# Window attention and FFN in one kernel: weight bits joined from a PSUM bank, a longer count for the turns, one copy at the end, a new table of offsets

## The chip, the cores and the metric

One core of one Trainium2 chip runs the whole program. Its engines are TensorE (PE, with its weight loads shown as PEld), VectorE (DVE), ScalarE (ACT), GpSimd (POOL) and SyncE (SP), which here issues nearly all DMAs. Each engine takes its own instructions in order and waits for the others through semaphores. The metric is device microseconds of one execution, as the median of three runs.

## The reference

`reference` computes attention over 8 batches and 8 heads of 64 columns, and feeds the result to a feed-forward network (FFN). Every head has 32 global and 512 local tokens. Global queries see all 544 keys; local queries see the 32 global keys and the local keys at most 32 places away.

```
s_g = scale * np.matmul(q_g, k_all.transpose(0, 1, 3, 2))
out_g = np.matmul(sm(s_g), v_all)
mask = np.abs(pos[:, None] - pos[None, :]) <= window
s_ll = np.where(mask, s_ll, -1000000000.0)
out_l = np.matmul(sm(np.concatenate([s_lg, s_ll], axis=-1)), np.concatenate([v_g, v_l], axis=2))
h = x @ w_in
g = h - np.tanh(h)
return (g @ w_out).astype(np.float32)
```

x is the attention output, 4352 rows of 512; w_in is 512 by 2048 and w_out 2048 by 512. Both weights come as 64-bit floats, the rest as 32-bit floats.

## The kernel before

**Precision.** Each factor of the FFN's matmuls is split into a rounded part and a remainder (hi and lo), and three products are added: hi by hi, hi by lo, lo by hi.

**Weights.** `add_weights` (L396) handles 32 pieces, 16 of w_in and 16 of w_out. A piece is loaded as 512 pairs of 32-bit words for each partition, into `wraw01` or, for every other piece, `first_q`. A buffer's next load waits until its piece has been joined. Four steps make one float of a pair: `rebias` on ACT (L429) rescales the upper word in place; `low` on DVE (L433) shifts the lower word by 29 places in place; `join` on DVE (L438) shifts the upper word by 3, ors both and writes `sq`; `high` on ACT (L364) rounds it into `w_in_hi` or `w_out_hi`, and `rest` (L444) subtracts that into `w_in_lo` or `w_out_lo`. Which engine subtracts, DVE or POOL, is the planner's choice.

**Attention.** Heads go in pairs, 32 in all, four to a batch. Pairs 0 to 3 are worked out by an older way: PE transposes keys and queries (L547), scores (L656), DVE finds peaks, ACT takes exponentials (L1111), POOL scales (L1117), PE transposes the probabilities (L1176), ACT or DVE stores them, and PE forms the products (L814). From pair 4 on the band scores come from L730, the exponentials from L1137, POOL scales (L1146), DVE turns blocks (L1152), DMAs put them in their places, and the products come from L814 up to pair 7 and L830 after. Values are loaded into one buffer, so a pair's values are loaded once the products before it are done. The scores of the global queries are made for two pairs at once (a quad, `L1030`, or `L972` from pair 8 on); their path is peaks (L982, L985), a swap of halves (L977), exponentials (L993), a second swap and reciprocal (L997, L998), scaling on POOL (L1003), and two turns on DVE, one for each head (L793 and L795), and then the products of the quad's first pair (L830).

**FFN.** Eight chunks of 512 local rows and a last one of 256 global rows. A step makes 128 hidden columns: 12 matmuls of 128 by 512 (L1219; the first four steps of batch 0 are written at L1245, so that they can begin with the first heads), tanh on ACT (L1227), a subtraction on DVE (L1230), rounding to `gates` (L364), the remainder (L1236, by DVE or POOL), and 12 more matmuls into the output (L1282). The hidden sums use PSUM banks 0 to 3, outputs 4 to 7, attention 0 to 2 from batch 1 on.

**Order.** Nothing is ordered by hand. `Order.run` is a planner: each operation states engines it may run on, with a duration and a penalty for each, a due time, what it reads and writes, and the banks it takes. The planner repeatedly takes the operation that could start first by its own reckoning. `lock` marks DVE operations that it will not overlap with POOL's. Due times, penalties and offsets come from the table `CFG`. When PE would be idle early on, the planner puts in matmuls without use, called fillers here (L1520). What it decides is fixed at build time: the chip sees plain queues, and banks are fixed with them.

Of the kernel before, what the change touches and what calls it, by code (L numbers as in the profile page):

```python
# [217 lines left out]
def kernel(ctx, tc, q_l, k_l, v_l, q_g, k_g, v_g, w_in, w_out, out):  # L218
    nc = tc.nc
    B, H, S, _ = q_l.shape  # L220
# [3 lines left out]
    DM, DFF = w_in.shape  # L224
# [11 lines left out]
    OWN = 8  # L236
# [94 lines left out]
    def bank(shape, j, dt=F32):  # L331
# [6 lines left out]
        elif len(shape) == 4:  # L338
# [4 lines left out]
    CFG = dict(a_g=-2.1233, a_kg=-0.0964, a_ph=-0.2641, a_qs=5.2608, a_w=-5.4882, a_wn=-5.0581, a_xg=150, d_g=3.6283, d_kg=1.9778, d_ph=50.4226,  # L343
               d_qh=26.732, d_qs=-7.1422, d_tg=0.8523, d_tp=37.2986, d_w=30.7139, d_wn=39.585, d_xg=38.7617, d_y=2.8076, gfirst=0, ho=5270.2449,
               hs=2156.5317, lag=1357.4346, last=1709.3, newb=2, p0=1360.6541, pen=53.0844, penp=52.559, s_g=-0.3344, s_w=0.027, step=4184.7811,
               step1=131.5084, lag0=-8364.46, hs0=1060.8452, tol=7.769536e-06, wd0=5841.993, wsp=-418.2128, xw=0.0005229852, o_ld0=7690.8676,
               o_tn0=177.2342, o_tg0=-8529.9354, o_s0=-8629.8545, o_sp0=-1339.9745, o_t0=-1524.9303, o_vl0=2302.8731, o_pv0=-5083.3973,
               wsp1=-52.8356, ho0=6811.9657, mw=0.141697, o_h0=-385.2625, hp=-7418.8823, bp0=8145.2771, bp1=-8139.4914, bp2=-3489.8108,
               bp3=-2305.7318, p_w=49.4081, p_kg=19.7546, mv=1.068302e-05, kd=2.127385e-05, a_sq=8.5297, o_gb=6064.0102, o_kl2=-2470.8967,
               o_ql2=2380.1114, o_kt2=930.5723, o_qt2=7843.6435, o_l2=-3985.7135, o_lp2=2466.9212, o_g2=-2616.5954, o_tg2=-354.9467,  # L350
               o_sq2=-3032.5223, o_vl2=-3610.1076, o_pv2=8733.5803, o_kl1=5682.2566, o_ql1=7667.6045, o_kt1=1958.0937, o_qt1=-6967.0531,
               o_l1=-6273.5988, o_lp1=7383.6579, o_g1=4840.8538, o_tg1=7460.9702, o_sq1=7629.0969, o_vl1=-2671.5821, o_pv1=-8776.7889,
               o_g0=-5078.2772, p_bd=49.2555)
# [4 lines left out]
    add = order.add  # L358
# [4 lines left out]
    def copy(e, dst, src):  # L363
        (nc.scalar.copy if e == "A" else eng[e].tensor_copy)(dst, src)  # L364
# [31 lines left out]
    def add_weights(n):  # L396
# [10 lines left out]
        box = {}  # L407
# [23 lines left out]
        def low(e, _):  # L431
            v = box["v"].bitcast(I32)
            nc.vector.tensor_scalar(v, v, 29, None, op0=ALU.logical_shift_right)  # L433

        def join(e, _):
            v, up = [box["raw"][:, :, k].bitcast(I32) for k in range(2)]
            box["v"] = flat
            nc.vector.scalar_tensor_tensor(box["v"].bitcast(I32), up, 3, v, op0=ALU.logical_shift_left, op1=ALU.bitwise_or)  # L438
# [61 lines left out]
    class Pair:  # L500
# [278 lines left out]
        def add_global_turn(self):  # L779
            for a in self.heads:  # L780
# [17 lines left out]
                add(("D", 1.65 if self.j >= OWN else 1.6), turn, self.due(self.C["o_tg"]), r=["pg0"], w=[f"hg{a.two}"])  # L798
# [391 lines left out]
    class Chunk:  # L1190
        def __init__(self, x, xkeys, n, name, dst, due):
            self.x, self.n, self.name, self.dst, self.due = x, n, name, dst, due
            self.hs = CFG["hs0"] if name == "b0" else CFG["hs"]
            self.per = 512 // n
            self.steps = NF // self.per
            self.xkeys = xkeys
            self.h, self.g, self.acc, self.final = {}, {}, None, False
# [69 lines left out]
        def add_out(self, s):  # L1267
# [31 lines left out]
            if last:  # L1299
                for tt in range(nt):  # L1300
# [14 lines left out]
                    if self.final and tt == nt - 1:  # L1315
                        def half(lo):
                            def fn(e, _, tt=tt, key=key):
                                copy(e, wraw[key[1]][:, lo:lo + DM // 2], self.acc[tt][:, lo:lo + DM // 2])
                            return fn
# [7 lines left out]
                    parts = [key, key + ("b",)] if self.final and tt == nt - 1 else [key]  # L1327
                    add(("S", 0.45 * k), out_dma(runs[:k]), due + 0.5, r=parts, w=[("out", self.name, tt)], xfer=0.78)
                    if runs[k:]:
                        add(("A", 0.45 * k), out_dma(runs[k:]), due + 0.5, r=parts, w=[("out", self.name, tt, 1)], xfer=0.78)  # L1330
# [183 lines left out]
    chunks[-1].final = True  # L1514
# [42 lines left out]
```

## Time and profile before

| | us |
|---|---|
| median of three runs | 920.47 |
| lowest and highest | 916.97, 920.97 |
| the profiled execution | 916.99 |
| its span in the trace | 915.2 |
| PE busy in the span | 895.0 |
| DVE busy | 550.6 |
| ACT busy | 386.2 |
| POOL busy | 204.3 |

The span runs from the first to the last instruction; the execution's own time is 1.8 us more. Times in the trace are counted from the span's start. A view by stretches gives the busy time of each engine between two moments; a timeline lists instructions with the idle time before them and what ended it; the chain of waits follows the last instruction back to what released it. A busy PE is not always one at work that is needed, since fillers count as busy, and its clock may be granted at one of two levels, 1.0 being 2.4 GHz and 0.5 being 1.2 GHz.

### The profile page before, as it was taken

The numbers are of one execution on the slowest core, as the hardware profiler recorded it, in microseconds if no ns is written. First come the engines' busy times: TensorE is split into PE (matmuls) and PEld (weight loads), VectorE is DVE, ScalarE is ACT, GpSimd is POOL, SyncE is SP. The second block draws the span as 40 slices with busy tenths as digits, with TensorE's granted clock in tenths as the row PEclk, the third lists the DMA queues.
The fourth block names the chain that finished last, engine by engine and source line by source line (L and its number), as shares of the span: only waits on it lengthen the run. The fifth ranks groups of instructions, "written<-read, shape, count | busy, mean of one in ns | idle before, by whom it ended". The sixth has DMA issues, their size and how long they took to land.

```text
span 915.2 us, 23456 instructions
## 1 busy us (share of the span) xinstructions
PE 895.0 (98%) x9109; PEld 720.6 (79%) x9109; DVE 550.6 (60%) x1916; ACT 386.2 (42%) x1078; POOL 204.3 (22%) x366
## 2 busy tenths in 40 slices
PE   8989999999999999999999999999999999999998
PEld 6757777787787878777787878777778878888896
DVE  6878878855848485575747485665847462222231
ACT  6976566433334343433334343533344332322221
POOL 5656654220113121221113121211102030000000
PEclk9999999999999999999999999999999999999999
DMA  9785674754545525554645536454555330100100
GB/s 202 181 211 172 182 185 117 179 123 105 123 105 134 144 58 128 128 111 110 127 107 131 136 65 147 120 110 101 124 120 129 94 93 1 47 1 1 45 2 23
DMA packets 286958, 101.13 MB, mean 110 GB/s; under 512 B 254848, under 2 KB 277376, under 8 KB 286848
## 3 DMA queue, kind: packets, MB, share of 16 engines
q1 hardware_dynamic: 284800, 98.53, 45.2%
q8 instruction: 71, 1.16, 0.6%
q10 hardware_dynamic: 2048, 1.11, 0.5%
q14 instruction: 39, 0.32, 0.1%
HBM read 76.01 MB, written 21.50 MB: 107 GB/s over the span
## 4 chain that ended last, share of the span: by engine, by line
PE 74%; DVE 16%; ACT 4%; DMA 2%; SPq 2%; issue 2%; POOL 0%; ACTq 0%; DVEq 0%; POOLq 0%
PE bank L1282 33%; PE bank L1219 31%; DVE turned L793 4%; PE bank L830 4%; PE bank L730 3%; DVE stats L977 2%; DVE t L1230 2%; SPq L752 1%; DVE sq L1152 1%; PE bank L972 1%; DVE sq L438 1%; DVE pg L982 1%; PE bank L1245 1%; ACT turned L364 1%; DVE turned L795 1%
## 5 line engine op out<-in xcount | busy, mean ns | idle before, releaser
L1282 PE MATMUL bank<-w_out_hi,gates 128*128 128x512 f32 x1088 | 299.3, 395 | 2.8 <-ACT gates L364 2.8
L1282 PEld LDWEIGHTS bank<-w_out_hi,gates 128*128 128x128 f32 x1088 | 200.8, 188 | 50.8 <-issue 5.0
L1230 DVE TENSOR_TENSOR t<-bank,t 128x512 f32<-128x512 f32 x136 | 92.9, 684 | 173.1 <-ACT t L1227 172.7
L1146 POOL TENSOR_SCALAR prob<-prob,stats 128x128 f32<-128x128 f32 x224 | 91.1, 425 | 457.6 <-DVE stats L1142 264.0
L1227 ACT ACTIVATE t<-bank 128x512 f32<-128x512 f32 x136 | 80.8, 596 | 234.1 <-PE bank L1219 233.7
L364 ACT CAST gates<-t 128x512 fp32r<-128x512 f32 x136 | 84.5, 622 | 197.1 <-PE bank L1282 126.0
L1282 PE MATMUL bank<-w_out_lo,gates 128*128 128x512 f32 x544 | 151.7, 393 | 0.1
L1236 DVE TENSOR_TENSOR gates<-t,gates 128x512 fp32r<-128x512 f32 x101 | 70.5, 698 | 100.0 <-PE bank L1282 91.2
L1219 PE MATMUL bank<-x_hi,w_in_hi 128*128 128x512 f32 x432 | 120.5, 395 | 0.0
L1282 PEld LDWEIGHTS bank<-w_out_lo,gates 128*128 128x128 f32 x544 | 102.5, 188 | 22.4 <-issue 0.3
L1219 PE MATMUL bank<-x_hi,w_in_lo 128*128 128x512 f32 x432 | 118.6, 390 | 0.0
L1219 PE MATMUL bank<-x_lo,w_in_hi 128*128 128x512 f32 x432 | 118.3, 390 | 0.0
L1219 PEld LDWEIGHTS bank<-x_lo,w_in_hi 128*128 128x128 f32 x432 | 81.0, 188 | 17.3 <-issue 0.2
L1219 PEld LDWEIGHTS bank<-x_hi,w_in_lo 128*128 128x128 f32 x432 | 80.6, 188 | 17.6 <-issue 0.2
L1219 PEld LDWEIGHTS bank<-x_hi,w_in_hi 128*128 128x128 f32 x432 | 79.6, 188 | 17.6 <-issue 0.6
L1137 ACT ACTIVATE prob<-prob,stats 128x128 f32<-128x128 f32 x224 | 86.9, 390 | 2.1 <-DVE stats L1132 2.0
L793 DVE STREAM_TRANSPOSE turned<-pg 32x96 f32<-32x96 f32 x288 | 77.5, 269 | 5.6
L1236 POOL TENSOR_TENSOR gates<-t,gates 128x512 fp32r<-128x512 f32 x35 | 46.1, 1319 | 47.2 <-PE bank L1282 25.7
L1152 DVE STREAM_TRANSPOSE sq<-prob 128x512 f32<-128x512 f32 x50 | 34.6, 703 | 33.5 <-POOL prob L1146 32.1
L1132 DVE CUSTOM_DVE_ANT_0 prob<-bank,band 128x128 f32<-128x128 f32 x224 | 49.4, 284 | 0.6 <-PE bank L730 0.5
L830 PEld LDWEIGHTS bank<-turned 128*32 128x32 f32 x3072 | 33.4, 111 | 13.1 <-DVE turned L795 8.5
L1137 ACT ACTIVATION_READ_ACCUMULATOR prob<-prob,stats 128x1 f32 x224 | 42.1, 188 | 0.0
(159 smaller groups left out, 935.4 us busy)
## 6 DMA issues: line engine op xcount, KB each, us to landing
moved<-sq SPq DMA_DIRECT2D x24, 512.0 KB, 3.0
turned<-in_v_l_dram SPq DMA_DIRECT2D x23, 512.0 KB, 5.5
turned<-in_v_l_dram SPq DMA_DIRECT2D x32, 256.0 KB, 3.4
out_dram<-wraw SPq DMA_DIRECT2D x32, 256.0 KB, 2.1
rawkq<-in_k_l_dram SPq DMA_DIRECT2D x112, 64.0 KB, 2.5
rawkq<-in_q_l_dram SPq DMA_DIRECT2D x112, 64.0 KB, 2.4
turned<-in_v_g_dram SPq DMA_DIRECT2D x48, 128.0 KB, 4.6
turned<-moved SPq DMA_DIRECT2D x48, 128.0 KB, 3.7
```

Source lines behind the costliest of these rows:

```text
L364: (nc.scalar.copy if e == "A" else eng[e].tensor_copy)(dst, src)
L793: nc.vector.transpose(win_g[G * g:G * g + G, a.two, 3 * x:3 * x + 3], view(pgh[r, a.two, G * (j + x):G * (j + x) + 1], [(3 * G, 3), (1, G)]))
L830: m = nc.tensor.matmul(y, win_v[:, NW * a.two + w, G * d:G * d + G], x, start=n == 0, stop=n == 7, skip_group_check=True)
L1132: nc.vector.tensor_tensor_reduce(out=x[:, t], in0=self.scores[:, t], in1=bands[0 if t == 0 else 2 if t == NT - 1 else 1], scale=-0.125, sc ...
L1137: nc.scalar.activation(x[:, t], x[:, t], AF.Exp, bias=self.st[:, t:t + 1], scale=-1.0, accum_out=self.st[:, 4 + t:5 + t])
L1146: nc.gpsimd.tensor_scalar(x[:, t], x[:, t], self.st[:, 8 + t:9 + t], 1.0, op0=ALU.mult, op1=ALU.mult)
L1152: nc.vector.transpose(z[:, :, self.two].rearrange("p n t c -> p t n c"), x[:, :, k * n * G:(k + 1) * n * G].rearrange("p t (n c) -> p t n ...
L1219: nc.tensor.matmul(self.h[s][:, j * n:(j + 1) * n], w[:, cc, f * P:(f + 1) * P], self.x()[xi](cc)[:, :n], start=part == 0 and cc == 0 and ...
L1227: nc.scalar.activation(tt_[q], self.h[s], AF.Tanh)
L1230: nc.vector.tensor_sub(tt_[q], self.h.pop(s), tt_[q])
L1236: eng[e].tensor_sub(gg[q][1], tt_[q].rearrange("p (k c) -> p k c", k=4), f32(gg[q][0]))
L1282: nc.tensor.matmul(self.acc[tt], g[:, j * nt + tt], low_out(f) if wi else w_out_hi[:, f], start=s == 0 and k == 1, stop=last and k == 3 * ...
```

## The change

Four things change. `low` no longer writes over the raw words: it takes a PSUM bank (any of the eight for the first eight pieces, later one of banks 0 to 3), writes the shifted bits there, and `join` reads them from it and gives it back. The planner's account is changed with it: `low` at 0.68 us instead of 0.48, `low`, `join` and DVE's subtraction no longer marked as locked against POOL, and the global turn from pair 8 on at 1.9 us instead of 1.65. The last chunk's last rows are copied out of PSUM by one instruction, where two copied a half each. And the table `CFG` has new values throughout, so the planner makes another order.

```diff
     def subtract(n, kind):
-        return [("P", (0.17 + n * 0.00218), 0.0), ("D", (n + 151) / 960, CFG.get("s_" + kind, PENP), True)]
+        return [("P", (0.17 + n * 0.00218), 0.0), ("D", (n + 151) / 960, CFG.get("s_" + kind, PENP), False)]
...
-        def low(e, _):
-            v = box["v"].bitcast(I32)
-            nc.vector.tensor_scalar(v, v, 29, None, op0=ALU.logical_shift_right)
+        def low(e, tags):
+            box["low"] = bank([P, 512], tags[low_]).bitcast(I32)
+            nc.vector.tensor_scalar(box["low"], box["v"].bitcast(I32), 29, None, op0=ALU.logical_shift_right)
...
-            nc.vector.scalar_tensor_tensor(box["v"].bitcast(I32), up, 3, v, op0=ALU.logical_shift_left, op1=ALU.bitwise_or)
+            nc.vector.scalar_tensor_tensor(box["v"].bitcast(I32), up, 3, box["low"], op0=ALU.logical_shift_left, op1=ALU.bitwise_or)
...
-            add(("D", 0.48), low, due, r=keys, w=keys, lock=True)
-            add(("D", 0.69), join, due, r=keys, w=[wj], lock=True)
+            low_ = ("low", n)
+            add(("D", 0.68), low, due, r=keys, w=[low_], alloc=[(low_, None if n < 8 else "h")])
+            add(("D", 0.69), join, due, r=keys + [low_], w=[wj], free=[(low_, 1)])
...
-                add(("D", 1.65 if self.j >= OWN else 1.6), turn, self.due(self.C["o_tg"]), r=["pg0"], w=[f"hg{a.two}"])
+                add(("D", 1.9 if self.j >= OWN else 1.6), turn, self.due(self.C["o_tg"]), r=["pg0"], w=[f"hg{a.two}"])
...
-                    if self.final and tt == nt - 1:
-                        def half(lo):
...
-                        add(("D", 0.42), half(DM // 2), due + 0.5, r=[acc], w=[key + ("b",)], res=[key], free=[(acc, 2)])
-                        add(("A", 0.37), half(0), due + 0.5, r=[acc], w=[key], free=[(acc, 2)])
-                    else:
-                        add(either(512, "y", True), out_copy, due + 0.5, r=[acc], w=[key], free=[(acc, 1)])
+                    add(either(512, "y", True), out_copy, due + 0.5, r=[acc], w=[key], free=[(acc, 1)])
...
-               hs=2156.5317, lag=1357.4346, last=1709.3, newb=2, p0=1360.6541, pen=53.0844, penp=52.559, s_g=-0.3344, s_w=0.027, step=4184.7811,
...
+               hs=1945.7008, lag=2058.0703, last=-656.3726, newb=2, p0=1174.4585, pen=-2.1431, penp=-16.7696, s_g=37.3966, s_w=10.8784,
```

**What the table does to the queues.** Counted over the whole program, all 136 gate subtractions (L1236) are on POOL, where 101 were on DVE; so are all 32 weight subtractions, where 9 were on DVE. The 28 copies of the global keys and four copies of the first global keys move from ACT to POOL. Four stores of the global turn, and the first store of the global keys and queries, move from ACT to DVE. There are 12 fillers instead of 21. Matmuls, exponentials and DMAs are as many as before.

On ACT, the rows ahead of the first tanh (`t_67<-bank`), before the change; `x_hi` is the products of the fourth pair, L429 is `rebias`, L1137 exponentials of batch 1:

```order
L1137 ACTIVATE prob_92,stats<-prob_92,stats 128x128 x4
L364 CAST w_out_hi<-sq 128x512
L364 CAST x_hi_75<-bank_105 128x256
L429 ACTIVATE wraw_64<-wraw_64 128x512
L364 CAST x_hi_75<-bank_101 128x256
L1137 ACTIVATE prob_93,stats<-prob_93,stats 128x128 x4
L364 CAST w_in_hi<-sq 128x4x128
L429 ACTIVATE first_q<-first_q 128x512
L1227 ACTIVATE t_67<-bank_102 128x512
L1227 ACTIVATE t_66<-bank_103 128x512
```

And after it:

```order
L428 ACTIVATE first_q<-first_q 128x512
L363 CAST x_hi_75<-bank_105 128x256
L363 CAST x_hi_75<-bank_104 128x256
L363 CAST w_out_hi<-sq 128x512
L428 ACTIVATE wraw_64<-wraw_64 128x512
L1227 ACTIVATE t_67<-bank_103 128x512
L363 CAST w_in_hi<-sq 128x4x128
L1227 ACTIVATE t_66<-bank_102 128x512
```

Both copies to `x_hi` now stand ahead of the rebias, and the eight exponentials behind the first tanh.

On SP, from the load of piece 8 into `wraw` to the load of piece 10 into it, before the change (`in_v_l`, `in_v_g` are values, `rawkq` raw keys and queries of batch 1):

```order
L418 DMA wraw_64<-in_moe_w_in_dram 128x4x256
L418 DMA first_q<-in_moe_w_out_dram 128x1024
L626 DMA turned<-in_v_l_dram 128x8x64
L626 DMA turned<-in_v_l_dram 64x8x64
L636 DMA turned<-in_v_g_dram 32x4x64 x2
L686 DMA rawkq<-in_k_l_dram 32x16x32 x4
L418 DMA wraw_64<-in_moe_w_in_dram 128x4x256
```

And after it (`qgt` is the global keys and queries):

```order
L417 DMA wraw_64<-in_moe_w_in_dram 128x4x256
L686 DMA rawkq<-in_q_l_dram 32x16x32 x4
L884 DMA qgt<-in_k_g_dram 32x4x32 x4
L626 DMA turned<-in_v_l_dram 128x8x64
L626 DMA turned<-in_v_l_dram 64x8x64
L636 DMA turned<-in_v_g_dram 32x4x64 x2
L417 DMA first_q<-in_moe_w_out_dram 128x1024
L884 DMA qgt<-in_q_g_dram 32x4x32 x4
L417 DMA wraw_64<-in_moe_w_in_dram 128x4x256
```

Counted from the first row of SP, four loads of raw keys fewer stand ahead of the load of piece 10.

On POOL, around the scaling for one quad of batch 2 (L1003), before the change:

```order
L1146 TENSOR_SCALAR prob_92<-prob_92,stats 128x128 x4
L1146 TENSOR_SCALAR prob_93<-prob_93,stats 128x128 x4
L1003 TENSOR_SCALAR pg<-pg,stats 128x288 x2
L1236 TENSOR_TENSOR gates<-t_67,gates 128x4x128
L1236 TENSOR_TENSOR gates<-t_66,gates 128x4x128
```

And after it:

```order
L1146 TENSOR_SCALAR prob_92<-prob_92,stats 128x128 x4
L1146 TENSOR_SCALAR prob_93<-prob_93,stats 128x128 x4
L1236 TENSOR_TENSOR gates<-t_66,gates 128x4x128
L1003 TENSOR_SCALAR pg<-pg,stats 128x288 x2
L1236 TENSOR_TENSOR gates<-t_67,gates 128x4x128
```

Around that quad, eight to ten gate subtractions (L1236) stand between one L1003 and the next, where one or two stood.

## Rows read from the trace of the kernel before

**Rows 1.** Busy us by stretch: length, then each engine (instructions), granted clock, DMA share, GB/s.

```profile
0.00:63.30 63.30, 53.90 (x453) 39.93 (x453) 47.96 (x202) 52.52 (x163) 34.25 (x67) 1.00 0.86 202
63.30:165.00 101.70, 99.91 (x757) 78.51 (x757) 87.25 (x276) 62.08 (x161) 59.55 (x70) 0.98 0.60 157
165.00:765.00 600.00, 595.21 (x7173) 478.26 (x7170) 378.26 (x1382) 234.77 (x694) 107.55 (x227) 1.00 0.50 116
```

**Rows 2.** Chain of waits in order of time, 52 to 58 us: start, us, what.

```profile
52.16 4.56 DMA wraw<-in_moe_w_in_dram
56.80 0.67 ACT wraw L429
```

**Rows 3.** Timeline of ACT: start us, us, instruction, count [idle before, releaser].

```profile
52.70 0.40 ACT L1137 ACTIVATE prob<-prob,stats 128x128 f32<-128x128 f32 x1
...
54.25 0.60 ACT L364 CAST w_out_hi<-sq 128x512 fp32r<-128x512 f32 x1
...
56.80 0.67 ACT L429 ACTIVATE wraw<-wraw 128x512 f32<-128x512 f32 x1 [1.68 <-DMA wraw<-in_moe_w_in_dram]
57.38 0.35 ACT L364 CAST x_hi<-bank 128x256 fp32r<-128x256 f32 x1
...
60.20 0.67 ACT L429 ACTIVATE first_q<-first_q 128x512 f32<-128x512 f32 x1
60.78 1.05 ACT L1227 ACTIVATE t<-bank 128x512 f32<-128x512 f32 x2
```

**Rows 4.** Timeline of PE around the first FFN steps, columns as in rows 3.

```profile
57.78 0.49 PE L1245 MATMUL bank<-x_hi,w_in_hi 128*128 128x512 f32 x1 [1.75 <-ACT x_hi L364]
...
63.46 1.30 PE L1282 MATMUL bank<-w_out_hi,gates 128*128 128x512 f32 x4 [2.43 <-ACT gates L364]
```

**Rows 5.** Granted clock of PE by stretch: length, PE busy, clock, DMA share, GB/s.

```profile
64.40:67.80 3.40, 3.40 (x10) 0.51 0.72 161
```

**Rows 6.** Timeline of the DMA queue of SP, columns as in rows 3.

```profile
49.06 3.00 SPq L686 DMA_DIRECT2D rawkq<-in_k_l_dram  x4
52.16 0.43 SPq L418 DMA_DIRECT2D wraw<-in_moe_w_in_dram  x1
```

**Rows 7.** Busy us of one line on DVE, L433, then L438, 0 to 165 us.

```profile
0.00:165.00 165.00, 19.91 (x32) 0.99 0.70 174
...
0.00:165.00 165.00, 26.83 (x32) 0.99 0.70 174
```

**Rows 8.** Line L438: duration ns min/median/max, first and last start.

```profile
L438 DVE SCALAR_TENSOR_TENSOR sq<-wraw x18: 650/694/1659, 8.8 to 148.5; 128x512 int32<-128x512 int32 x18
```

**Rows 9.** Groups by line and form, DVE, 0 to 165 us: busy, mean ns | idle.

```profile
L433 DVE TENSOR_SCALAR wraw<-wraw 128x512 int32<-128x512 int32 x18 | 11.7, 648 | 2.4 <-DMA wraw<-in_moe_w_out_dram 1.9 <-DMA wraw<-in_moe_w_in_dram 0.4
...
L364 DVE COPY first_q<-bank 128x512 f32<-128x512 f32 x4 | 2.7, 682 | 3.9 <-PE bank L547 3.9
```

**Rows 10.** Page, costliest groups: busy us, mean ns of one | idle before, releaser.

```profile
L1236 DVE TENSOR_TENSOR gates<-t,gates 128x512 fp32r<-128x512 f32 x101 | 70.5, 698 | 100.0 <-PE bank L1282 91.2
...
L1236 POOL TENSOR_TENSOR gates<-t,gates 128x512 fp32r<-128x512 f32 x35 | 46.1, 1319 | 47.2 <-PE bank L1282 25.7
```

**Rows 11.** Waits of PE: us in total, times, longest.

```profile
PE bank L830 <- DVE turned L795: 3.9, 11, 0.6
```

**Rows 12.** Timeline of one quad in batch 2, all engines, columns as in rows 3.

```profile
278.69 0.42 PE L972 MATMUL bank<-kw,qgt 64*32 64x256 f32 x4
...
283.17 1.13 DVE L977 COPY stats<-stats 32x2 f32<-32x2 f32 x4
...
289.62 0.20 DVE L795 STREAM_TRANSPOSE turned<-pg 32x32 f32<-32x32 f32 x1
...
289.88 1.33 PE L830 MATMUL bank<-turned 128*32 128x64 f32 x105 [0.27 <-DVE turned L795]
```

**Rows 13.** Timeline of the last rows' copies, columns as in rows 3.

```profile
909.61 0.59 ACT L364 COPY wraw<-bank 128x512 f32<-128x512 f32 x1 [4.42 <-PE bank L1282]
...
911.45 0.37 ACT L364 COPY wraw<-bank 128x256 f32<-128x256 f32 x1 [1.25 <-DVE wraw L364]
```

More of the change, by code (lines that the diff above doesn't have):

```diff
@@ new lines @@
+    CFG = dict(a_g=-20, a_kg=8.6471, a_ph=-0.3776, a_qs=3.1395, a_w=0.1186, a_wn=0.3468, a_xg=106.4499, d_g=3.1804, d_kg=30.2528, d_ph=13.5028,
+               d_qh=26.732, d_qs=-2.8448, d_tg=-7.2746, d_tp=19.0976, d_w=27.3757, d_wn=73.5687, d_xg=31.5443, d_y=19.0351, gfirst=0, ho=4086.9099,
+               hs=1945.7008, lag=2058.0703, last=-656.3726, newb=2, p0=1174.4585, pen=-2.1431, penp=-16.7696, s_g=37.3966, s_w=10.8784,
+               step=4056.6186, step1=117.929, lag0=-6898.385, hs0=174.1645, tol=0.0001449392, wd0=3738.22, wsp=-399.3218, xw=0.07263301,
+               o_ld0=6998.8548, o_tn0=-70.3794, o_tg0=4900.3517, o_s0=-8488.5413, o_sp0=-1339.9745, o_t0=-7480.9842, o_vl0=-4568.2292,
+               o_pv0=-6980.563, wsp1=-266.4844, ho0=4731.2006, mw=0.2696114, o_h0=9000, hp=-9000, bp0=8995.7209, bp1=-7509.0482, bp2=-3805.4551,
+               bp3=-9000, p_w=150, p_kg=-0.4636, mv=0.0001195388, kd=3.441514e-05, a_sq=8.5297, o_gb=8757.2134, o_kl2=-2217.8445, o_ql2=7034.0784,
+               o_kt2=-7538.1981, o_qt2=-1378.049, o_l2=-5351.7965, o_lp2=-2940.782, o_g2=-2834.6403, o_tg2=-1206.1443, o_sq2=-696.1794,
+               o_vl2=5851.8969, o_pv2=8097.3484, o_kl1=2328.5123, o_ql1=5480.9611, o_kt1=-1133.8937, o_qt1=-1536.1301, o_l1=-8243.7002,
+               o_lp1=4742.1478, o_g1=7959.6348, o_tg1=7293.7765, o_sq1=6170.1166, o_vl1=-3483.3411, o_pv1=310.4111, o_g0=-5056.3219, p_bd=33.4845)
@@ L429, in rebias @@
             nc.scalar.activation(up, up, AF.Prelu, scale=2.0 ** -112, alpha=-2.0 ** 32)
-        def low(e, _):
-            v = box["v"].bitcast(I32)
-            nc.vector.tensor_scalar(v, v, 29, None, op0=ALU.logical_shift_right)
+        def low(e, tags):
+            box["low"] = bank([P, 512], tags[low_]).bitcast(I32)
+            nc.vector.tensor_scalar(box["low"], box["v"].bitcast(I32), 29, None, op0=ALU.logical_shift_right)
         def join(e, _):
-            v, up = [box["raw"][:, :, k].bitcast(I32) for k in range(2)]
+            up = box["raw"][:, :, 1].bitcast(I32)
             box["v"] = flat
-            nc.vector.scalar_tensor_tensor(box["v"].bitcast(I32), up, 3, v, op0=ALU.logical_shift_left, op1=ALU.bitwise_or)
+            nc.vector.scalar_tensor_tensor(box["v"].bitcast(I32), up, 3, box["low"], op0=ALU.logical_shift_left, op1=ALU.bitwise_or)
         def high(e, _):
@@ L1196, in __init__ @@
             self.xkeys = xkeys
-            self.h, self.g, self.acc, self.final = {}, {}, None, False
+            self.h, self.g, self.acc = {}, {}, None
         def add_hidden(self, s):
@@ L1313, in out_dma @@
                         return fn
-                    if self.final and tt == nt - 1:
-                        def half(lo):
-                            def fn(e, _, tt=tt, key=key):
-                                copy(e, wraw[key[1]][:, lo:lo + DM // 2], self.acc[tt][:, lo:lo + DM // 2])
-                            return fn
-                        add(("D", 0.42), half(DM // 2), due + 0.5, r=[acc], w=[key + ("b",)], res=[key], free=[(acc, 2)])
-                        add(("A", 0.37), half(0), due + 0.5, r=[acc], w=[key], free=[(acc, 2)])
-                    else:
-                        add(either(512, "y", True), out_copy, due + 0.5, r=[acc], w=[key], free=[(acc, 1)])
+                    add(either(512, "y", True), out_copy, due + 0.5, r=[acc], w=[key], free=[(acc, 1)])
                     runs = self.dst(tt)
                     k = max(1, len(runs) // 2)
-                    parts = [key, key + ("b",)] if self.final and tt == nt - 1 else [key]
-                    add(("S", 0.45 * k), out_dma(runs[:k]), due + 0.5, r=parts, w=[("out", self.name, tt)], xfer=0.78)
+                    add(("S", 0.45 * k), out_dma(runs[:k]), due + 0.5, r=[key], w=[("out", self.name, tt)], xfer=0.78)
                     if runs[k:]:
-                        add(("A", 0.45 * k), out_dma(runs[k:]), due + 0.5, r=parts, w=[("out", self.name, tt, 1)], xfer=0.78)
+                        add(("A", 0.45 * k), out_dma(runs[k:]), due + 0.5, r=[key], w=[("out", self.name, tt, 1)], xfer=0.78)
     def local_rows(b):
```

11 lines of the change are left out of this document (removed).

## The prediction

> **What bounds the kernel now.** I read the stretches first [rows 1]. From 63.3 us on PE is nearly always at work: 99.9 of 101.7 us, then 595.2 of 600. What PE does there is the same in both kernels, so only idle time and bad time can be won. Before 63.3 us PE works 53.9 us, part of it fillers: the four pairs of batch 0 arrive slower than PE takes them. DVE is the busiest other engine from 63.3 to 165 us, at 87.3 of 101.7 us, and ACT before that, at 52.5 of 63.3. So three places count: when the first FFN output begins, whether batch 1's attention can follow an earlier start, and the small waits of the long middle.
>
> The first place is a chain. SP issues the load of weight piece 10 at 52.16 us, it lands 4.56 us later, and only then does ACT go on with the rebias [rows 2]. ACT had sat idle 1.68 us for it, and the second copy to `x_hi`, which owes nothing to that weight, stands behind it in ACT's queue until 57.38 [rows 3]. PE waits 1.75 us for that copy, and after six fillers another 2.43 us for the first gates, which it gets at 63.46 [rows 4]. Just after this wait the granted clock is 0.51 for 3.4 us, the 1.2 GHz level [rows 5].
>
> **The change part by part.** My sum goes against the profiled execution, 916.99 us (span 915.2 and 1.8 around it); the median of the runs, 920.47, stands 3.5 above it.
>
> *The first FFN steps.* ACT's queue ahead of the first tanh gets shorter. Eight exponentials go behind it: four take from 52.70 to 54.25, so 0.39 each and 3.1 in all [rows 3]. Four stores of the global turn go to DVE, each like a copy to `x_hi` at 0.35 [rows 3]: 1.4. Thirteen smaller copies go to POOL or DVE; no row here prices them alone, they lie between 0 and 0.35, and I take 0.17: 2.2. One rebias and one weight rounding less come to 1.2 (60.20 to 60.78 us, and 0.60 at 54.25) [rows 3]. That is 7.9 us. The chain holds back a part. On SP four loads of raw keys, 3.0 us, leave the place ahead of piece 10 [rows 6], so its load is issued near 49.2 and lands near 53.7 at the earliest; the rebias and then the tanh follow at 54.4, not 60.78: 6.4 us earlier. The copies to `x_hi` stand ahead of that rebias now and do not wait for it. But `wraw` must be free for the load, and DVE's queue ahead of that join is longer by two PSUM stores and the dearer shift. I take 4.5 of the 6.4; bounds 0 and 7.9.
>
> *The slow clock.* 3.4 us at half speed lose 1.7 [rows 5]. In the new order PE has a global score and one filler between its last early step and the first output, and gates come sooner after it, so I take the 2.43 us idle before it away, and the 1.7 with it. Bounds 0 and 1.7; if the wait stays, so may the slow stretch.
>
> *The shift in PSUM.* In SBUF the shift takes 0.65 on average and, with the join, 19.9 and 26.8 us for 32 pieces [rows 7, 9]. A DVE copy from PSUM of the same size takes 0.68 [rows 9], which is my price for a shift into it: 21.8. The join is 0.69 at the median and 1.66 at worst [rows 8]; it is stretched where POOL works beside it. If that ends, 32 joins are 22.2, and the two together 44.0 instead of 46.7, 2.7 less; if the join stays stretched they are 48.6, 1.9 more. The Trainium skill, "SBUF — State Buffer", section "Who interferes with whom", says that a DVE instruction with two SBUF inputs has to take turns with a POOL instruction that reads SBUF, and one with a single SBUF input outside the two-port modes does not. By that rule the join is freed and the sum is the one with 2.7 less; the spread from 0.69 to 1.66 [rows 8] agrees with it, but no row here shows a join with one input from PSUM. DVE also hands nine weight subtractions to POOL, like a gate subtraction at 0.70 [rows 10]: 6.3 less. So DVE has up to 9.0 us less to do by 165 us, from which some 3.5 for stores taken from ACT go off: 5.5.
>
> *Batch 1 follows or not.* PE would be 6.2 us ahead at the first outputs. Batch 1's attention is DVE's work, at 86% in that stretch [rows 1], and with 5.5 us less it can be nearly as much earlier. I let 1.5 of the 6.2 be given back; bounds 0 and 6.2.
>
> *The long middle.* PE waits 11 times for the last global turn, 3.9 us in all [rows 11]. The quad at 278.69 shows why: scores to last turn take 11.1 us, of which a swap of statistics is 1.13 where POOL works beside it, and PE is there 0.27 us sooner than the turn [rows 12]. The planner's longer count puts 48 FFN matmuls between each L972 and its products where there were 48 or 44. DVE no longer has a gate subtraction between, and POOL's subtractions lie before and behind L1003. So I take 3.5 of the 3.9 away; bounds 0 and 3.9.
>
> *Gate subtractions on POOL.* 101 go from 0.70 on DVE to 1.32 on POOL [rows 10]; 133 us more on an engine that is busy 107.6 of 600 us in the middle [rows 1]. The steps alternate, 2.7 us of hidden and 2.7 of output matmuls, and a step's remainder is needed two steps after its buffer comes free, so the 0.62 is hidden by some 8 us of matmuls. Without that cover, each costs 0.62. I take 0.
>
> *The last rows.* The two halves did not run together: ACT's ended at 911.82 after 1.25 us of waiting for DVE's [rows 13]. One copy takes 0.59 [rows 13] and from the same moment, 910.99, would end at 911.58. I take 0.2 less; bounds 0 and 0.3.
>
> Sum: −4.5 −1.7 +1.5 −3.5 −0.2 = −8.4, so 908.6 against the profiled execution, and 912.1 against the median. I say **910**, between them, since I can't tell which of the two the new runs will be like.
>
> **Rivals.** *The start is given back.* Batch 1's attention ends when it ended before, and PE, 6.2 us early, waits for it near 165 us. For it speaks DVE's 86%; against it the 5.5 us less. Then only the middle and the end are left: −3.7, or −2 if the middle keeps half its waits: 915 against the profiled execution, 918 against the median. The same comes out if the join stays stretched, which would be the change not doing what it says.
>
> *POOL becomes the late one (slower than before).* POOL's queue is in order: a gate subtraction that waits for its buffer holds up L1003 and L1146 behind it. Its place is the path from L972 to the products, twelve quads. If one subtraction of 1.32 lies in it late, and both swaps stay stretched by some 0.5, a path of 11.1 becomes 13.4 against about 11.5 us of PE's work: 1.9 each, 23 us in all in place of 3.9, and a start of −4.7 left: 916.99 + 19 − 5 = 931. It decides from a wait of 0.7 us per quad (4.7 and 3.9 over 12). Against it: in the new queue the subtraction ahead of L1003 belongs to a step whose buffer comes free about when L972 begins, and L1003 is wanted 6 us later.
>
> *More than forecast.* The 7.9 us of ACT all count and nothing is given back: −7.9 −1.7 −3.9 −0.3 = −13.8: 903.
>
> **How the numbers follow.** The forecast has 0.58, the start given back 0.22, POOL late 0.10, more than forecast 0.10. The range 902 to 921 takes in the forecast, what is given back against either level, and the better case; POOL late stays out. About 0.5%, 4.6 us, is what a measurement of this kernel can tell from no change. Against the median, the forecast and the better case are faster, save a small part of the forecast near 916; what is given back is mostly the same: faster 0.64, same 0.25, slower 0.11.
>
> **What would show it.** Right: the first tanh between 54 and 58 us, the first output matmul before 60, no stretch at 1.2 GHz after it, L433's successor at 0.68 and its join at 0.69 throughout, and L830 without a wait for L795. The start given back would show as PE idle between 140 and 170 us. POOL late would show as a wait of L830 or L1152 for L1003 or L1146, with L1236 just ahead on POOL. Wrong altogether: PE's idle time after 63 us above the 1.8 and 4.8 us of the two stretches [rows 1], with a releaser that is none of these, such as a PSUM bank held by a shift whose join is late.

## The result, and the profile after

| | before | after |
|---|---|---|
| median, us | 920.28 | 905.22 |
| lowest and highest of 4 | 916.97, 920.97 | 904.15, 907.01 |
| profiled execution | 916.99 | 905.91 |
| its span | 915.2 | 904.1 |

The ratio is 0.9847, with a 95% interval of 0.9827 to 0.9867. The forecast of 910 named the direction and its range held the time, but the gain is 15.1 us between medians, where 8.4 were summed. Between the profiled executions it is 11.1. The other 4.0 come from which executions were profiled: that of before was 3.3 below its median, that of after 0.7 above.

The same stretches as in [rows 1], after: length, busy time of PE, PEld, DVE, ACT and POOL, granted clock, DMA share, GB/s.

```profile
0.00:63.30 63.30, 57.10 (x455) 42.84 (x456) 49.28 (x206) 48.03 (x139) 36.46 (x73) 0.92 0.85 197
63.30:165.00 101.70, 101.46 (x850) 80.11 (x850) 85.40 (x291) 63.63 (x167) 64.92 (x87) 1.00 0.68 176
165.00:765.00 600.00, 599.22 (x7115) 482.01 (x7114) 327.87 (x1293) 226.08 (x672) 206.54 (x322) 1.00 0.48 113
```

Length less busy PE is PE's idle time. It falls from 9.4 to 6.2 us in the first stretch, from 1.8 to 0.2 in the second and from 4.8 to 0.8 in the third. After 765 us it is 4.2 both times. That is 8.8 less idle time. PE's busy time falls by 2.3, from 895.0 to 892.7: the fillers, 12 instead of 21, fall from 7.1 to 4.7 us, the scores of batch 0 (L656) rise from 7.1 to 10.2, since two of their four groups lie in the slow stretches shown below, and the rest is spread over the other lines. Together these are the 11.1.

The waits of PE from 165 to 765 us (us in total, times, longest) are down to one line, where [rows 11] had eleven waits on the last turn:

```profile
PE bank L1282 <- ACT gates L363: 0.6, 1, 0.6
```

The shift and the join, L432 and L437 now (duration ns min/median/max, first and last start); the join is to be held against [rows 8]:

```profile
L432 DVE TENSOR_SCALAR bank<-wraw x18: 675/694/697, 8.7 to 139.1; 128x512 int32<-128x512 int32 x18
...
L437 DVE SCALAR_TENSOR_TENSOR sq<-wraw,bank x18: 680/689/702, 9.5 to 139.9; 128x512 int32<-128x512 int32 x18
```

The start on SP, ACT and PE (timelines: start, us, instruction, count, idle before and releaser):

```profile
51.74 0.39 SPq L417 DMA_DIRECT2D wraw<-in_moe_w_in_dram  x1
...
55.90 0.37 ACT L363 CAST x_hi<-bank 128x256 fp32r<-128x256 f32 x1 [0.66 <-PE bank L814]
...
58.37 0.60 ACT L1227 ACTIVATE t<-bank 128x512 f32<-128x512 f32 x1 [0.98 <-PE bank L1245]
...
60.63 1.19 PE L1282 MATMUL bank<-w_out_hi,gates 128*128 128x512 f32 x4 [0.26 <-ACT gates L363]
```

And three stretches, columns as above:

```profile
7.80:11.20 3.40, 2.82 (x16) 2.74 (x16) 2.83 (x9) 1.30 (x2) 0.16 (x1) 0.52 1.15 282
38.80:45.20 6.40, 6.22 (x31) 4.73 (x32) 5.08 (x21) 5.07 (x14) 4.42 (x7) 0.50 0.93 225
63.30:68.00 4.70, 4.70 (x22) 3.81 (x22) 3.57 (x12) 3.54 (x14) 3.76 (x9) 1.00 0.60 157
```

Piece 10 is loaded only 0.4 us sooner than in [rows 6]. Still, the copy to `x_hi` comes 1.5 us sooner than in [rows 3], the first tanh 2.4 and the first output 2.8 [rows 4]. Both ACT rows now wait for PE and not for a weight. The slow stretch after the first output [rows 5] is gone, but two others stand ahead of it, 3.4 us at 7.8 and 6.4 us at 38.8, where the kernel before had none.

### The profile page after: what moved, and what is told of

It is laid out like the page before. It is cut to its first block, busy times and chain, and to the rows that moved or that the text cites. A ratio compares the mean times of both kernels' runs of the same rounds, so it can differ in the third digit from the quotient of the medians.

```text
span 904.1 us, 23449 instructions
## 1 busy us (share of the span) xinstructions
PE 892.7 (99%) x9100; PEld 719.8 (80%) x9100; DVE 481.7 (53%) x1820; ACT 372.5 (41%) x1035; POOL 338.9 (37%) x504
## 4 chain that ended last, share of the span: by engine, by line
PE 92%; DVE 4%; ACT 2%; issue 1%; DMA 1%; POOL 0%; ACTq 0%; DVEq 0%; POOLq 0%
PE bank L1282 40%; PE bank L1219 39%; PE bank L830 4%; PE bank L730 3%; PE bank L814 2%; PE bank L1245 1%; PE bank L656 1%; PE bank L1176 1%; PE bank L972 1%; DVE turned L793 1%; DVE stats L977 1%; DMA raw<-in_q_l_dram 1%; DVE t L1230 0%; ACT prob L1137 0%; PE bank L547 0%
## 5 line engine op out<-in xcount | busy, mean ns | idle before, releaser
L1236 POOL TENSOR_TENSOR gates<-t,gates 128x512 fp32r<-128x512 f32 x136 | 175.1, 1288 | 394.0 <-PE bank L1282 245.7
L1230 DVE TENSOR_TENSOR t<-bank,t 128x512 f32<-128x512 f32 x136 | 92.8, 684 | 238.8 <-ACT t L1227 238.3
L363 ACT CAST gates<-t 128x512 fp32r<-128x512 f32 x136 | 84.3, 622 | 166.9 <-PE bank L1282 92.8
L1219 PE MATMUL bank<-x_hi,w_in_hi 128*128 128x512 f32 x432 | 123.4, 401 | 0.0
L1146 POOL TENSOR_SCALAR prob<-prob,stats 128x128 f32<-128x128 f32 x224 | 79.0, 372 | 82.5 <-DVE stats L1142 43.7
L1137 ACT ACTIVATE prob<-prob,stats 128x128 f32<-128x128 f32 x224 | 86.9, 390 | 22.8 <-DVE stats L1132 22.8
L1137 ACT ACTIVATION_READ_ACCUMULATOR prob<-prob,stats 128x1 f32 x224 | 42.1, 188 | 0.0
L830 PE MATMUL bank<-turned 128*32 128x32 f32 (+1 forms) x3072 | 37.2, 206 | 0.1
```

The lines of the kernel that those rows point to most:

```text
L830: m = nc.tensor.matmul(y, win_v[:, NW * a.two + w, G * d:G * d + G], x, start=n == 0, stop=n == 7, skip_group_check=True)
L1137: nc.scalar.activation(x[:, t], x[:, t], AF.Exp, bias=self.st[:, t:t + 1], scale=-1.0, accum_out=self.st[:, 4 + t:5 + t])
L1146: nc.gpsimd.tensor_scalar(x[:, t], x[:, t], self.st[:, 8 + t:9 + t], 1.0, op0=ALU.mult, op1=ALU.mult)
L1219: nc.tensor.matmul(self.h[s][:, j * n:(j + 1) * n], w[:, cc, f * P:(f + 1) * P], self.x()[xi](cc)[:, :n], start=part == 0 and cc == 0 and ...
L1230: nc.vector.tensor_sub(tt_[q], self.h.pop(s), tt_[q])
L1236: eng[e].tensor_sub(gg[q][1], tt_[q].rearrange("p (k c) -> p k c", k=4), f32(gg[q][0]))
```

## The experiments

In nine of the twelve kernels below, each engine's queue is that of the kernel it comes from, instruction for instruction, except for the edit named: the planner's plan is kept and only what is emitted from it changes. In the three others the planner orders anew, and the text says so. Each is compared by its ratio to the kernel before on the same chip; a difference to the changed kernel is the difference of the ratios (after: 0.9847) times 920.

**The shift back in SBUF, same queues.**

```diff
-            box["low"] = bank([P, 512], tags[low_]).bitcast(I32)
-            nc.vector.tensor_scalar(box["low"], box["v"].bitcast(I32), 29, None, op0=ALU.logical_shift_right)
+            box["low"] = box["v"].bitcast(I32)
+            nc.vector.tensor_scalar(box["low"], box["low"], 29, None, op0=ALU.logical_shift_right)
```

> The changed kernel with its queues kept instruction for instruction, but the shift writes over the raw words in SBUF again, and the join reads both inputs from there. Theory A, the PSUM input is what frees the join: the 32 joins go from 22.0 us back above 24, some at 1 us and more where POOL works beside them, the shifts from 22.1 to 18 to 20, and the sum is about as large as in the changed kernel; batch 1 gets back some of its waits, and the time rises by 0.5 to 2 us over 905.2. Rival B, the place of the shift is worth nothing or costs: DVE's sum falls by 2 or more, and the time is the same within 1 us or lower.

Measured: 0.9970 (0.9953 to 0.9987), 11.3 us more than the changed kernel. Nearly the whole gain is lost, far more than either theory gave. Shift and join (duration rows as above):

```profile
L432 DVE TENSOR_SCALAR wraw<-wraw x18: 397/628/1495, 8.8 to 148.5; 128x512 int32<-128x512 int32 x18
...
L437 DVE SCALAR_TENSOR_TENSOR sq<-first_q x14: 687/928/1596, 18.7 to 132.6; 128x512 int32<-128x512 int32 x14
```

Their busy time on DVE from 0 to 165 us, the shift and then the join, columns as in [rows 7]:

```profile
0.00:165.00 165.00, 24.98 (x32) 0.99 0.70 174
...
0.00:165.00 165.00, 32.17 (x32) 0.99 0.70 174
```

The two take 57.1 us, against 44.2 with PSUM. In SBUF the shift is quicker at best (0.40) and 1.5 at worst, and the join reaches 1.6; through PSUM no join exceeds 0.70 although POOL works beside 23 of the 32 for 30% of their time or more. POOL is stretched too: one scaling of L1146 takes up to 0.91, against 0.37. PE is idle for 6.1 us from 63.3 to 165 us, against 0.2 with PSUM. Five of its waits after 60 us follow; the four from 77 us on lie where batch 1's attention is due, and each is for DVE:

```profile
60.61 1.19 PE L1282 MATMUL bank<-w_out_hi,gates 128*128 128x512 f32 x4 [0.87 <-ACT gates L363]
...
77.41 1.19 PE L1219 MATMUL bank<-x_hi,w_in_hi 128*128 128x512 f32 x4 [1.58 <-DVE stats L1132]
...
94.49 1.20 PE L814 MATMUL bank<-turned 128*64 128x160 f32 x14 [0.55 <-DVE turned L786]
96.38 1.26 PE L814 MATMUL bank<-turned 128*64 128x160 f32 x16 [0.69 <-DVE t L1230]
...
103.75 1.14 PE L730 MATMUL bank<-kw,hi 64*32 64x128 f32 x62 [1.03 <-DVE xg L856]
```

The first output comes at 60.61, as with PSUM (60.63). So in this order the PSUM shift does nothing for the first output, and decides whether batch 1 follows.

**Half of the pieces in SBUF.** Pieces with an even number shift in place, the others in PSUM.

> The changed kernel with its queues kept, but every other piece (the 18 in wraw or, late, all with an even number: 16 of 32) shifted in SBUF. Theory A, each SBUF piece costs DVE its stretch (13 us for 32 of them) and batch 1 hangs on DVE: shift and join sum to about 50.5 us, and the time rises by 3 to 6 us over 905.2, about half of the 10 that all 32 cost. Rival B, DVE has slack that the first pieces use up: under 1.5 us. Rival C, one late piece is enough to start a chain of waits: 8 us or more.

Measured: 0.9874 (0.9847 to 0.9902), 2.5 us more than the changed kernel, between theories A and B; the two intervals overlap (the changed kernel's ends at 0.9867), so the time alone doesn't settle it. PE's idle time from 63.3 to 165 us lies in between too: 3.1 us, against 0.2 and 6.1. L432 and L437 sum to 22.4 and 25.0 us, 3.2 over the changed kernel, where all 32 cost 13. So the stretch is not a fixed price for a piece; why half of them cost so much less than half was not settled.

**The gate subtractions on POOL in the old order, and on DVE in the new one.** One word changes, `eng[e]` to `nc.gpsimd` in the kernel before, and to `nc.vector` in the changed one:

```diff
-                eng[e].tensor_sub(gg[q][1], tt_[q].rearrange("p (k c) -> p k c", k=4), f32(gg[q][0]))
+                nc.gpsimd.tensor_sub(gg[q][1], tt_[q].rearrange("p (k c) -> p k c", k=4), f32(gg[q][0]))
```

> The kernel before with its queues kept in their order, except that all 136 gate subtractions go to POOL at the place in the program where 101 stood on DVE. Theory A, the engine of the subtractions decides: with 70 us less on DVE the waits of PE for the last global turn (3.9 us) fall below 1 us, and the time falls by 3 to 5 us. Rival B, the order decides (44 FFN matmuls between the scores of a quad and its products in five of twelve quads): 1.5 us or more of these waits stay, and the time falls by at most 2 us. Rival C, POOL is late: PE waits for L1236, L1003 or L1146, and the time rises.

Measured: 1.0037 (1.0022 to 1.0053), slower. The waits of PE from 175 us on grew:

```profile
PE bank L830 <- DVE turned L795: 6.9, 11, 0.7
```

No theory holds as it stands: 70 us less on DVE brought nothing (A), the waits stay but the time rises (B), and PE waits for L795 and not for POOL (C). In the quad that answers to [rows 12], scores at 282.84, the last turn ends after 11.53 us instead of 11.13; in the quads between it is 12.44 instead of 12.20. So the subtractions on DVE were not what kept the last turn late there.

The run also shows whether moving the gate subtractions makes the shift and the join dearer. Busy time from 0 to 165 us of L1236 in the kernel before (DVE, then POOL), and of the shift and the join in this run, columns as in [rows 7]:

```profile
0.00:165.00 165.00, 0.00 (x0) 21.52 (x16) 0.99 0.70 174
...
0.00:165.00 165.00, 20.13 (x32) 0.99 0.70 173
...
0.00:165.00 165.00, 26.70 (x32) 0.99 0.70 173
```

While weights are joined, every gate subtraction of the kernel before is on POOL already; all 101 on DVE come after 165 us. So moving them leaves shift and join as they were: 46.8 us here, 46.7 in [rows 7].

> The changed kernel with its queues kept in their order, but all 136 gate subtractions on DVE at the same place in the program. Theory A, the engine decides: DVE gets 95 us more, PE waits again for the last global turn, 3 us or more in all, batch 1 loses 1 to 3 us, and the time rises by 4 to 8 us over 905.2. Rival B, the order of the changed kernel with 48 matmuls in between is enough: the time rises by at most 1.5 us. Rival C, the shorter subtraction (0.70 in place of 1.29) helps: the time falls.

Measured: 0.9901 (0.9877 to 0.9925), 5 us more than the changed kernel. From 165 us on:

```profile
PE bank L830 <- DVE turned L795: 1.8, 4, 0.5
```

Theory A holds for the time, not for the waits: four quads wait again, 1.8 us and not 3 or more; part of the loss lies in batch 1, where PE is idle for 1.8 us from 63.3 to 165 us and not 0.2. So the move to POOL costs 3.4 us in the old order and brings 5.0 in the new one, and the new order keeps 9 of its 14 us without it. In the changed kernel a quad looks so (DVE's swaps and last turn, POOL's subtraction and scaling, PE's products):

```profile
269.19 0.42 PE L972 MATMUL bank<-kw,qgt 64*32 64x256 f32 x4
...
271.47 1.29 POOL L1236 TENSOR_TENSOR gates<-t,gates 128x512 fp32r<-128x512 f32 x1 [0.29 <-POOL prob L1146]
...
271.74 2.00 DVE L977 COPY stats<-stats 32x2 f32<-32x2 f32 x4
...
276.44 0.99 POOL L1003 TENSOR_SCALAR pg<-pg,stats 128x288 f32<-128x288 f32 x2 [2.88 <-DVE stats L998]
...
280.80 0.20 DVE L795 STREAM_TRANSPOSE turned<-pg 32x32 f32<-32x32 f32 x1
...
281.06 1.13 PE L830 MATMUL bank<-turned 128*32 128x64 f32 x91
```

The swap takes 2.00: the first of its four copies ends when POOL's subtraction does, and the next two lie beside two copies that are now on POOL. In [rows 12] the swap took 1.13. The path from the scores to the last turn's end is 11.81 us, longer than the 11.13 of [rows 12]. Four FFN matmuls more (0.9 us) stand on PE in between, so the products begin at 11.87 without a wait. In the quads between, which had 48 matmuls before and after, the path fell from 12.20 to 11.36.

**The turn counted at 1.65 again**, in the planner's account only (here the planner orders anew).

> The changed kernel with one number put back: the global turn counted at 1.65 us, not 1.9. Theory A, as the prediction had it, the longer count keeps the turn ahead of PE: waits for L795 come back, 1 to 3 us. Rival B, the count does next to nothing here, since ten of twelve quads still have 48 matmuls between and only the last two get 52 and 44 in place of 56 and 48: no more than 0.5 us of waits for L795, and the time within 1 us of 905.2.

Measured: 0.9867 (0.9841 to 0.9892), 1.8 us more, which the intervals don't tell from the changed kernel; no wait for L795 in the trace. Rival B holds: the count isn't what put 48 matmuls there.

**Code alone and table alone** (the planner orders anew in both).

> The changed code (shift into PSUM, no locks, turn counted at 1.9, one last copy) with the table of offsets of the kernel before; the planner makes its own order: 118 gate subtractions on DVE, 24 fillers, 44 matmuls in four quads. Theory A, the PSUM shift by itself takes the stretch from shift and join: the two sum to 44 us in place of 46.7, and the time falls by 1 to 3 us against the kernel before, no more, since POOL has few subtractions here and the stretch was small. Rival B, the PSUM shift is worth its 8.7 us in any order: the time falls by 6 us or more. The start stays as before under both (first output between 62 and 65 us).

Measured: 1.0275 (1.0253 to 1.0298). Both theories fall. Shift and join are 43.7 us, as theory A said, but this order is bad for batch 1 and its first output comes at 66.7, later than both said. Of PE's waits, that on a DMA for turned blocks is the longest, and the granted clock is 0.56 from 163 to 198 us, which adds to the time.

```profile
PE bank L814 <- DMA turned<-sq: 11.7, 2, 11.3
```

> The code of the kernel before (shift in SBUF, locks, turn at 1.65, two half copies) with the new table: all subtractions on POOL, 20 fillers. Theory A, the table needs the PSUM shift: shift and join sum to more than 50 us or wait for POOL in the planner's account, batch 1 is late, and the time is 915 or more; the long middle still has no waits for L795, since 48 matmuls stand between in all quads but the last. Rival B, the table brings the gain by itself: 905 to 910.

Measured: 1.0441 (1.0418 to 1.0464). Theory A's direction holds, not its size: shift and join are 56.6 us, and PE waits 14.1 us in two waits on a DMA of batch 1; from 168 to 217 us the granted clock is 0.51. Waits for L795 are 4.1 us in code alone and 0.3 in table alone. A table fits the account that it was made for; these two runs show that neither half works alone as the planner then orders it, but price neither, since each made an order of its own.

**The start made earlier in the kernel before: ACT's order.** The second copy to `x_hi` goes ahead of the rebias, four exponentials behind the first gates (line numbers are 8 higher here).

> The kernel before with two steps moved in ACT's queue and nothing else: the second copy to x_hi goes ahead of the rebias of piece 10, and the four exponentials between that copy and the first tanh go behind the first gates. Theory A, the copy behind the rebias and the exponentials set the first output: x_hi near 55.1 in place of 57.38, the first output 1.5 to 3 us earlier than 63.46, the time 1 to 3 us lower. Rival B, the load of piece 10 sets it: the rounding of that weight still stands ahead of the tanh, and the first output comes within 1 us of 63.46.

Measured: 0.9985 (0.9970 to 1.0001), at most a small gain. The first output comes at 62.67, 0.8 earlier. PE waits for it as long as before, and yet no slow stretch follows it; one comes at 92.8, after PE's next long wait. PE at the first output, PE and DVE at batch 1's first products, and the clock there (a stretch, columns as after the change), in this kernel:

```profile
62.67 1.19 PE L1290 MATMUL bank<-w_out_hi,gates 128*128 128x512 f32 x4 [2.46 <-ACT gates L372]
...
85.89 1.07 PE L1227 MATMUL bank<-x_hi,w_in_hi 128*128 128x512 f32 x4
...
90.95 0.46 PE L822 MATMUL bank<-turned 128*64 128x160 f32 x2 [2.18 <-DMA turned<-x_lo1b]
...
95.19 1.19 PE L1227 MATMUL bank<-x_hi,w_in_hi 128*128 128x512 f32 x2
...
87.46 1.15 DVE L441 TENSOR_SCALAR wraw<-wraw 128x512 int32<-128x512 int32 x1
88.65 1.64 DVE L446 SCALAR_TENSOR_TENSOR sq<-wraw 128x512 int32<-128x512 int32 x1
90.31 0.30 DVE L794 STREAM_TRANSPOSE turned<-pg 32x128 f32<-32x128 f32 x1
...
93.00:96.00 3.00, 3.00 (x19) 2.43 (x17) 2.47 (x9) 1.81 (x4) 2.58 (x4) 0.50 1.04 205
```

And the same two FFN steps on PE, and the shift and join on DVE between them, in the kernel before:

```profile
88.33 1.07 PE L1219 MATMUL bank<-x_hi,w_in_hi 128*128 128x512 f32 x4
...
94.47 0.72 PE L1219 MATMUL bank<-x_hi,w_in_hi 128*128 128x512 f32 x2
...
87.76 1.23 DVE L433 TENSOR_SCALAR wraw<-wraw 128x512 int32<-128x512 int32 x1
89.03 1.66 DVE L438 SCALAR_TENSOR_TENSOR sq<-wraw 128x512 int32<-128x512 int32 x1
```

PE was 2.4 us ahead at 85.89 and 0.7 behind at 95.19. Two waits, for a DMA of turned blocks and for a turn on DVE, took 2.1 us more than the one of 0.59 in the kernel before; the slow stretch took the rest. DVE was never ahead by as much: the stretched shift and join that stand ahead of the turns began only 0.3 us sooner than in the kernel before. This is one execution; over all of them the time is 1.4 us lower, with an interval from 2.8 lower to 0.1 higher.

**The start made earlier in the kernel before: the load.** Four loads of raw keys go behind the load of piece 10.

> The kernel before with one step moved in SP's queue: four loads of raw keys go behind the load of piece 10. Theory A, the load sets the chain: issued near 49.8 in place of 52.16, rebias near 54.6, x_hi near 55.2, the first output 2 us earlier, the time 1.5 to 2.5 us lower. Rival B, the queue of ACT holds the gain back or the raw keys come too late for batch 1: the time within 1 us of the kernel before, or above it.

Measured: 0.9993 (0.9980 to 1.0007). Line numbers are 7 higher here. The load was issued at 49.37 and the copy to `x_hi` came at 56.04, 1.3 us sooner, but the next weight's rebias stands ahead of the tanh too and waits for its own load. The first output comes only 0.15 us sooner, after a longer wait than before, and the granted clock is 0.50 for 5.5 us after it:

```profile
60.58 0.68 ACT L436 ACTIVATE first_q<-first_q 128x512 f32<-128x512 f32 x1 [1.46 <-DMA first_q<-in_moe_w_out_dram]
61.15 1.08 ACT L1234 ACTIVATE t<-bank 128x512 f32<-128x512 f32 x2
...
63.31 2.07 PE L1289 MATMUL bank<-w_out_hi,gates 128*128 128x512 f32 x4 [3.48 <-ACT gates L371]
```

Theory A got its load and its copy and lost the rest there; rival B's result holds.

**The start put back in the changed kernel.**

> The changed kernel with its start put back: four loads of raw keys go ahead of the load of piece 10 on SP, and the second copy to x_hi goes behind the rebias of that piece on ACT. Under both theories the first output comes 2 to 3 us later than 60.63. Theory A, the start counts here, since batch 1 has slack: the end is later by as much, 2 to 3 us. Rival B, batch 1's attention sets the time from 90 us on, as it does where the same start is made earlier in the kernel before: PE waits less in batch 1, and the end is later by under 1 us.

Measured: 0.9890 (0.9864 to 0.9917), 4 us more than the changed kernel, and a span longer by 3.2. PE waits 3.91 us for `x_hi`, and the first output comes 2.9 us later:

```profile
58.05 0.79 PE L1245 MATMUL bank<-x_hi,w_in_hi 128*128 128x512 f32 x1 [3.91 <-ACT x_hi L363]
...
63.49 1.21 PE L1282 MATMUL bank<-w_out_hi,gates 128*128 128x512 f32 x4
```

Theory A holds: here a late start stays to the end, where the profiled execution of the kernel before gave an early one back.

**Two reciprocals earlier on DVE in the changed kernel.**

> The changed kernel with two steps of DVE moved: the two reciprocals for the third pair (L671, L672) go ahead of a join and of one subtraction into x_lo. PE waits 1.18 and 0.18 us for them at 36.87 and 39.10. Theory A, DVE's queue sets this wait: about 0.6 us less idle of PE there, and the time falls by 0.3 to 1 us, if the start counts. Rival B, the exponentials on ACT set it, or the join that is late costs as much: the time is the same within 0.3 us or higher.

Measured: 0.9842 (0.9814 to 0.9870), the same as the changed kernel. The two waits fall from 1.4 to 0.9 us in all. But PE now waits for the join that came later, as rival B had it, and the changed kernel has no such wait:

```profile
59.42 0.64 PE L1030 MATMUL bank<-kw,qgt 128*64 128x512 f32 x1 [1.45 <-DVE sq L437]
```

**The last rows in two halves.**

> The changed kernel with the last rows copied in two halves again, DVE's first. Theory A, as the prediction had it, the halves cost 0.2 us: from the last matmul's start to the last output transfer 1.29 us or more, against 1.24 with one copy. Rival B, the order of the two copies decides and not their number: the same within 0.05 us.

Measured (one execution): from the last matmul's start to the last transfer 1.29 us, 901.25 to 902.54. DVE's half, ACT's half and the transfer:

```profile
901.68 0.42 DVE L363 COPY wraw<-bank 128x256 f32<-128x256 f32 x1 [6.88 <-PE bank L1282]
902.13 0.37 ACT L363 COPY wraw<-bank 128x256 f32<-128x256 f32 x1 [1.25 <-DVE wraw L363]
902.54 0.85 ACTq L1316 DMA_DIRECT2D out_dram<-wraw  x2
```

The one copy of the changed kernel, whose last matmul starts at 899.51:

```profile
900.13 0.59 ACT L363 COPY wraw<-bank 128x512 f32<-128x512 f32 x1 [0.98 <-PE bank L1282]
900.75 0.85 ACTq L1312 DMA_DIRECT2D out_dram<-wraw  x2
```

The time to the transfer is 1.29 us against 1.24, so one copy brings 0.05 us, not 0.2, as far as single executions tell; the kernel before has 1.29 too (910.56 to 911.85). ACT begins 0.62 us after the last matmul's start, DVE after 0.43.

## Why the prediction was right, and where it was not

Expected and measured in the profiled executions, in us. Idle time of PE is taken from the stretches; the 2.3 that PE is less busy are put to the start, where the fillers and the slow stretches lie; that is an allocation and not a reading.

| | expected | measured |
|---|---|---|
| first FFN steps and slow clock | −4.5 −1.7 = −6.2 | −3.2 −2.3 = −5.5 |
| batch 1 | +1.5 | −1.6 |
| long middle | −3.5 | −4.0 |
| last rows | −0.2 | −0.05 |
| sum | −8.4 | −11.1 |

The direction and the range came true, but two terms that missed offset each other in part: the start brought less than the sum had, and batch 1 gave nothing back. Undone one at a time, the PSUM shift (11.3), the subtractions on POOL (5.0) and the earlier start (4.0) come to 20 us, more than the 14 that the whole change brings by the ratio. So they overlap, and no list of terms that are simply added can be read off the runs.

**The start** (4.5 expected). The first output came 2.8 us earlier. Two of the prediction's own signs were missed: the first tanh at 58.37, not before 58, and the first output at 60.63, not before 60. The step that failed is the load: piece 10 was issued at 51.74, not near 49.2, since SP's queue ahead of it ran later. What counted is ACT's queue, as the sum had it: the tanh no longer stands behind the rounding of piece 10 and the next rebias. The earlier load in the kernel before points the same way from the other side, since it only moved the wait to the next rebias; no run moves these two alone.

**The slow clock** (1.7). The stretch behind the first output is gone, as said. But this execution has two others at half speed, in which PE is busy 2.8 and 6.2 us, so they lose about 4.5 (an estimate: half of that). Ahead of the first PE had waited 1.3 us for raw queries, ahead of the second 1.2 and 0.2 near 37 and 39. So in this execution the term has the wrong sign: the slow clock cost more than before, not 1.7 less. Nor is the reason borne out, that the stretch goes with the wait: with ACT's order changed in the kernel before, the wait of 2.46 us stayed and the stretch behind it did not come. The executions with a mean clock of 1.000 took 904.15 and 904.53, those with 0.993 and 0.996 took 905.91 and 907.01. What decides in which execution a slow stretch comes was not settled.

**The shift in PSUM and batch 1** (1.5 given back). Nothing was given back. The sizes were right (44.0 expected for shift and join, 44.2 measured), and the joins kept their length. The rule of the Trainium skill that the prediction weighed ("SBUF — State Buffer", section "Who interferes with whom") agrees with the join: with one input from PSUM it shows no stretch. The same section says that the shift's kind (`tensor_scalar`) can also take the port pair that DVE shares with POOL, in its quick modes; the SBUF run agrees, with a shift of 0.40 us drawn out to 1.5. What was mis-sized is the base. The sum compared 44.0 with the 46.7 of the kernel before, but in the new queues the same steps in SBUF cost 57.1. The gate subtractions are not the reason, since until 165 us all of them were on POOL before the change too. What differs there is the order, the nine weight subtractions and the copies of global keys that came to POOL: POOL works beside 23 of the 32 joins for 30% of their time or more, where it was 15, and those 23 take 1.13 us on average in SBUF. Which of these counts most was not separated. So PSUM is worth 13 us of DVE and 11 of time in this order, and the rival that the start is given back is what happens without it: the SBUF run shows it, and the ACT run agrees. No run has the PSUM shift in the old order with its queues kept.

**The long middle** (3.5). All eleven waits for L795 are gone, as said, and PE's idle time fell by 4.0. The reason was half wrong. The longer count did not set the 48 matmuls; taking it back leaves them. The table did, as code alone (4.1 us of waits) and table alone (0.3) show, together with the subtractions' engine: in the old order POOL's subtractions lengthen the path (11.13 to 11.53), in the new one DVE's do (11.81 to 12.21). With them on DVE the new order leaves PE idle for 2.4 us there, so of the 4.0 the engine has 1.6 and the order the rest.

**Gate subtractions on POOL** (0). No PE wait names them, so the 0.62 each are hidden. The rival that POOL is late did not come, but its stretch did: a swap of 2.00, covered by PE's work, with the last turn ended 0.06 us before the products begin.

**The last rows** (0.2). 0.05; ACT's later start was left out.

## What to carry to other kernels

Price a step in the company that it will have after the change, not in that which it has now: a DVE step that reads two operands from SBUF gets dearer where a new order puts POOL's work beside it, and here a PSUM operand took it out of that. Look when moved work runs before you blame it: the gate subtractions that moved came after the last join. An earlier start is worth something only if the next stage can follow; undo it in both kernels to see. An engine change can lose in one order and win in another, so keep the queues fixed when you want its price, and take it in the order that it is meant for.

## What the runs showed of the hardware

A join of 128x512 with one input in PSUM takes 0.68 to 0.70 us, though POOL works beside 23 of 32 for 30% of their time or more; with both in SBUF it takes 0.69 to 1.60 in the same queues. A shift in place in SBUF takes 0.40 to 1.50, into PSUM 0.67 to 0.75. Four small swaps of statistics (32x2) take 0.68 us in one place and 2.00 beside a subtraction and two copies on POOL. The changed kernel had the granted clock at half speed in two stretches of the first 46 us in one execution, and a mean clock of 1.000 in two others. A wait of PE of 2.4 us ahead of the first output was followed by 3.4 us at half speed in one kernel, and one of 2.5 us in another was not.
